# Split k weight copies, three more filler matmuls, a new load order and new issue lists in a fused attention and gMLP block

## Chip, core and metric

One NeuronCore of a Trainium2 chip runs the whole program. The metric is the device time of one execution in microseconds, here the median of several executions. The profile is of one more execution, read as time from the first to the last instruction of the program (the span).

## What is computed

The input x is 2048 tokens by 448 features in bf16. A pre-norm attention block is followed by a pre-norm gMLP block, each with a residual sum:

```python
qkv = layernorm(x) @ wqkv                 # 16 heads of 28
idx = pos[:, None] - 2 * arange(8)        # each token sees 8 tokens, 2 apart
o   = softmax(q . k[idx] * 28**-0.5, masked where idx < 0) . v[idx]
h   = x + o @ wo
z   = gelu(layernorm(h) @ w_in)           # 1792 wide: z1 and z2, 896 each
g   = w_sp @ layernorm(z2) + b_sp         # w_sp mixes the 2048 tokens
out = h + (z1 * g) @ w_out
```

## The kernel before, in words

Tokens lie in 16 blocks of 128. Blocks u and u+8 form unit u, so there are eight units, worked from 7 down to 0. One half of the partitions of `xh` holds the features of the low tokens and the other half those of the high ones, so most matmuls run as pairs on 64 rows each.

The stages, with the lines of the profile:

- **First layernorm** (`ln_unit`, L647 to L710): `bn_stats` and `bn_aggr` per block on DVE (L656, L657), the root `rs1_u` on POOL (L646, L647) or ACT (L668, L669), the normalised blocks `nrm1_b` into `tring` on DVE (L676). Units 7, 6 and 5 are transposed by PE (`tT1_u`, L692, seven matmuls) and copied to `xh` (`ev1_u`, L641 or L643). Units 4 to 0 are transposed by DMA (`tD1_u`, L683).
- **Weights of q and k**: loaded into a staging area in `z2p` and copied into `wpd` with 32 columns a head (`cpq`, `cpk`, L641 on ACT, L643 on DVE). v needs only the copies `cpv` between partition halves.
- **Projections and attention**: `mmq`, `mmk` (L783, chunks 3, 2, 1, 0 of 128, 128, 256 and 512 tokens), `mmv` (L823), logits `mml` (L858), row sums `mmr` (L886), values `mmo` (L911), output projection `mmy` (L964).
- **gMLP**: `mmz2` (L984), `mmz1` (L1028), the mixing over tokens `g` (L1064, nearly half of PE's time), the output `wo` (L1093).

The order of work is not that of the source. The functions add about 680 tasks, and a table of numbers, `SEQ`, gives for each engine (SP, POOL, DVE, ACT, PE) the list of its tasks. `Planner.replay` walks the five lists, hands out PSUM banks and buffers and emits the instructions. Semaphore waits follow from what each task reads and writes, so a change of a list changes what stands behind what on an engine, and which PSUM banks a task gets. DMAs are issued from SP's list and, at the start, from ACT's.

Two things ahead of the projections matter below. `c_warm` (L614) fills the operand of the filler matmuls `f0` (L635), which keep PE busy until the first transposes; `c_wo0` (L627) clears the area of the output weights. Both run on DVE.

The planner keeps a count of PE instructions, two for each matmul (a weight load and the matmul), since PE's instructions arrive in blocks. The count at which a block is asked for and the one at which it must be there are written so:

```python
CHUNK, ASK, NEED = 256, 118, 434
...
a, b = self.CHUNK * len(self.asks) + self.ASK, self.CHUNK * self.k_need + self.NEED
```

Block boundary k therefore stands at PE instruction 434 + 256 k, which is matmul 217 + 128 k, and its block is asked for 158 matmuls earlier.

Of the kernel before, what the change touches and what calls it, by code (L numbers as in the profile page):

```python
# [32 lines left out]

SCALE = DH ** (-0.5)
SEQ = (
# [30 lines left out]
)  # L66
NBANKS = 8
NE = 2
# [310 lines left out]
def bass_sequential_preLN__sliding_local_dilated__mixer_gmlp__prompt_kernel(  # L379
# [18 lines left out]
    with contextlib.ExitStack() as top:  # L398
# [71 lines left out]
        r_st = {p: [Res("st%s%d" % (p, n)) for n in range(2)] for p in "kqv"}  # L470
# [159 lines left out]
        def fill(name, n, deps=()):  # L630
            fb = []

            def em():
                for _ in range(n):
                    iss("pe", lambda e: e.matmul(psum[:, fb[0] * 512:fb[0] * 512 + 512], warm[:, 0:128], warm[:, :]),  # L635
                        reads=[r_warm], writes=[r_bank[fb[0]]])
            return add(name, "pe", 0.216 * n, em, deps=[c_warm] + list(deps), acq=[("ps", 1, fb)], rel=[("ps", fb)], mode="F", nmm=n)
# [12 lines left out]
        def ln_unit(u, which, src_deps, ev_deps):  # L650
# [11 lines left out]
            def em_r():  # L662
# [4 lines left out]
                else:  # L667
                    iss("act", lambda e: e.activation(dst, var, AF.Ln, bias=epst[:, 0:1]), reads=rr + [r_eps], writes=rr)  # L668
                    iss("act", lambda e: e.activation(dst, dst, AF.Exp, scale=-0.5), reads=rr, writes=rr)  # L669
            tr = add("rs%d_%d" % (which, u), "pool", 1.1, em_r, deps=tb + [c_nhalf, c_eps],  # L670
                     epoch=0 if which == 1 else None, alts={"pool": 1.1, "act": 0.36} if which == 1 else None)
            tk.append(tr)
            tn, h = [], []
            for n, b in enumerate(bl):
# [32 lines left out]
        for u in range(NU - 1, -1, -1):  # L707
# [3 lines left out]
                               [r_xh[NU - 1]], [r_xpad[1]])], 0.2, eng="dve", deps=[t_xh[NU - 1]])  # L711

        fill("f0", 15)
        c_kpad = cst("c_kpad", [(lambda e: e.memset(kT[:, :, :, HALO + ST:XW], 0.0), [], [r_kend]),
                                (lambda e: e.memset(kT[:, 0, :, 0:HALO], 0.0), [], [r_kh]),
                                (lambda e: e.memset(qT[:, :, :, 0:2], 0.0), [], [r_qend]),
# [22 lines left out]

        t_cp = {}  # L740
        for p in "kq":
            for j in range(2 if p == "q" else 1):
                nh = 8 if p == "q" else 16
                for n, (h, q) in enumerate(((0, 0), (0, 1), (1, 0), (1, 1))):
                    tk = []
                    nb = 4 - q
                    ne = nb * nh * DH

                    def em(p=p, h=h, q=q, j=j, n=n, nb=nb, nh=nh, tk=tk):
                        copy(tk[0].eng, wpd[p][64 * h:64 * h + 64, q:NC7:2, 256 * j:256 * j + 32 * nh].rearrange("p c (h d) -> p c h d", d=32)[:, :, :, 0:DH],  # L750
                             w_st[p][64 * q:64 * q + 64, 0:nb, 224 * j:224 * j + nh * DH].rearrange("p c (h d) -> p c h d", d=DH),
                             r_st[p], [r_w[p][j][n]] if p == "q" else [r_w[p][0][n], r_w[p][1][n]])
                    t = add("cp%s%d%d%d" % (p, j, h, q), "dve", dve4x(ne), em, deps=t_w[p] + [c_wp[p]], alts={"dve": dve4x(ne), "act": act_c(ne)})
                    tk.append(t)
                    for jj in ((j,) if p == "q" else (0, 1)):
                        t_cp.setdefault((p, jj), []).append(t)
        t_cp["v", 0] = cross("cpv", wv, r_w["v"], t_w["v"], D)

# [405 lines left out]
```

## Time and profile before

| | us |
|---|---|
| median of 3 executions | 242.88 |
| lowest and highest | 242.75, 243.28 |
| the profiled execution, its own time | 242.73 |
| its span | 240.9 |
| PE busy, of the span | 233.1 (97%) |
| DVE busy | 140.3 (58%) |
| ACT busy | 96.1 (40%) |
| POOL busy | 26.9 (11%) |

The profiled execution is 0.15 us under the median. Its own time stands 1.8 us over its span. To read it: the time is the time at which PE starts real work, plus PE's stream, plus PE's gaps, plus the last addition and store. A gap of PE is put down in the profile to the engine that ended it, or to "issue" when it waited for nothing that the profile shows.

### The profile page before, as it was taken

The page shows a single profiled execution, that of the slowest core. Times are in us where ns is not written, and L with a number is a line of the kernel's source. Part 1 is how long each engine was busy: PE and PEld are TensorE (multiplying, and loading weights), DVE is VectorE, ACT ScalarE, POOL GpSimd, SP SyncE. Part 2 cuts the span into 40 slices and gives each one's busy share as a digit, 9 for nine tenths or more (in the row PEclk, how much of TensorE's full clock was granted, in tenths as well). Part 3 has the DMA queues.
Part 4 walks back from the last instruction along what each step waited for, and adds up shares of the span by engine and source line. Part 5 has one row for each costly group of instructions (what it writes and reads, how often), then busy time and mean ns, then how long its engine had stood idle before and what let it go on. Part 6 is the DMA issues. An engine that isn't in the chain of part 4 may idle for free.

```text
span 240.9 us, 6695 instructions
## 1 busy us (share of the span) xinstructions
PE 233.1 (97%) x3009; PEld 119.9 (50%) x3019; DVE 140.3 (58%) x280; ACT 96.1 (40%) x113; POOL 26.9 (11%) x66
## 2 busy tenths in 40 slices
PE   7898999999999999999999999999999999999995
PEld 2486865456554544554444444444444444444453
DVE  5999959378999899788810050253101436554443
ACT  2996988889899947764730000000000000000000
POOL 4062000002014321304600000000000000000000
PEclk9999999999999999999999999999999999999999
DMA  7949575574213557987632733350000000010122
GB/s 213 337 106 103 112 125 95 97 127 53 44 22 77 109 85 174 169 133 117 141 76 58 174 68 65 85 46 0 0 0 3 0 0 19 20 60 0 38 93 78
DMA packets 54628, 20.01 MB, mean 83 GB/s; under 512 B 46792, under 2 KB 54472, under 8 KB 54600
## 3 DMA queue, kind: packets, MB, share of 16 engines
q1 hardware_dynamic: 53496, 18.67, 39.6%
q10 hardware_dynamic: 1104, 0.92, 1.3%
q8 instruction: 23, 0.38, 0.7%
q14 instruction: 5, 0.04, 0.1%
HBM read 6.37 MB, written 1.84 MB: 34 GB/s over the span
## 4 chain that ended last, share of the span: by engine, by line
PE 88%; DVE 5%; DMA 2%; issue 1%; POOL 1%; ACT 1%; SPq 0%
PE psum L1064 40%; PE psum L783 11%; PE psum L1093 9%; PE psum L984 8%; PE psum L964 5%; PE psum L823 5%; PE psum L1028 4%; PE psum L858 2%; PE psum L911 2%; DMA x_tm<-in_A_x_dram 2%; DVE z2p L1014 2%; PE psum L886 1%; DVE st L1000 1%; DVE tring L676 1%; POOL rs L647 1%
## 5 line engine op out<-in xcount | busy, mean ns | idle before, releaser
L1073 DVE TENSOR_TENSOR ub<-psum,reg 128x512 bf16<-128x512 f32 x28 | 18.9, 687 | 68.7 <-PE psum L1064 66.4
L1064 PE MATMUL psum<-reg,z2p 128*128 128x512 bf16 x220 | 49.4, 379 | 0.2
L1064 PE MATMUL psum<-wspT_lo,z2p 128*128 128x512 bf16 x218 | 48.5, 379 | 0.4 <-DVE z2p L1014 0.2
L1064 PEld LDWEIGHTS psum<-wspT_lo,z2p 128*128 128x128 bf16 x224 | 21.8, 98 | 26.6 <-issue 0.4
L1064 PEld LDWEIGHTS psum<-reg,z2p 128*128 128x128 bf16 x224 | 21.9, 98 | 26.2
L783 PE MATMUL psum<-xh,reg 64*128 64x128 bf16 (+2 forms) x448 | 26.0, 270 | 0.2
L1093 PE MATMUL psum<-reg 128*128 128x448 bf16 (+2 forms) x119 | 22.2, 341 | 0.1
L984 PE MATMUL psum<-w_in,xh 64*128 64x448 bf16 x224 | 22.2, 349 | 0.0
L1028 PE MATMUL psum<-xh,w_in 64*128 64x512 bf16 x196 | 21.8, 376 | 0.0
L641 ACT ACTIVATE reg<-psum 128x896 bf16<-128x896 f32 (+2 forms) x25 | 20.0, 844 | 1.9 <-PE psum L783 1.0
L783 PEld LDWEIGHTS psum<-xh,reg 64*128 64x128 bf16 x448 | 16.8, 94 | 7.8 <-issue 0.8
L656 DVE BATCH_NORM_STATS2 st<-x_tm 128x6 f32<-128x448 bf16 x32 | 19.6, 612 | 1.4 <-DMA x_tm<-in_A_x_dram 1.2
L1000 DVE BATCH_NORM_STATS2 st<-z2p 128x6 f32<-128x448 bf16 x32 | 17.5, 611 | 3.1 <-ACT z2p L994 3.1
L870 ACT ACTIVATE reg<-psum 128x928 bf16<-128x928 f32 x18 | 16.2, 939 | 4.1 <-PE psum L858 4.1
L646 POOL TENSOR_SCALAR rs<-mv 128x2 f32<-128x2 f32 x19 | 7.5, 393 | 88.4 <-DVE mv L657 70.2
L1038 ACT ACTIVATE reg<-psum 128x1024 bf16<-128x1024 f32 x14 | 13.6, 1029 | 8.0 <-PE psum L1028 8.0
L1093 PEld LDWEIGHTS psum<-reg 128*128 128x128 bf16 x119 | 11.4, 98 | 10.4
L994 ACT ACTIVATE z2p<-psum 128x896 bf16<-128x896 f32 x16 | 14.2, 916 | 5.6 <-PE psum L984 5.6
L1103 DVE TENSOR_TENSOR tring<-psum,x_tm 128x448 bf16<-128x448 f32 (+2 forms) x17 | 10.1, 596 | 10.2 <-PE psum L1093 10.1
L984 PEld LDWEIGHTS psum<-w_in,xh 64*128 64x128 bf16 x224 | 10.6, 94 | 10.4 <-issue 0.4
L929 DVE TENSOR_TENSOR reg<-psum,reg 128x912 bf16<-128x912 f32 x9 | 11.1, 1235 | 7.2 <-ACT reg L921 6.6
L1028 PEld LDWEIGHTS psum<-xh,w_in 64*128 64x128 bf16 x196 | 9.5, 94 | 11.5
(63 smaller groups left out, 205.9 us busy)
## 6 DMA issues: line engine op xcount, KB each, us to landing
x_tm<-in_A_x_dram SPq DMA_DIRECT2D x15, 112.0 KB, 4.2
out_dram<-tring SPq DMA_DIRECT2D x15, 112.0 KB, 1.7
w_in<-in_B_w_in_dram SPq DMA_DIRECT2D x2, 448.0 KB, 4.5
reg<-in_B_w_out_dram SPq DMA_DIRECT2D x1, 784.0 KB, 6.0
z2p<-in_A_wqkv_dram ACTq DMA_DIRECT2D x2, 336.0 KB, 4.5
reg<-in_B_b_sp_dram SPq DMA_DIRECT2D x1, 512.0 KB, 4.6
w_in<-in_B_w_in_dram SPq DMA_DIRECT2D x2, 224.0 KB, 4.3
reg<-in_A_wo_dram SPq DMA_DIRECT2D x4, 98.0 KB
```

The lines of the kernel that those rows point to most:

```text
L641: iss("act", lambda e: e.activation(dst, src, AF.Copy), reads=rd, writes=wr)
L656: iss("dve", lambda e: e.bn_stats(st[:, b, :], x_tm[:, b, :]), reads=[r_x[b]], writes=[rl[b]])
L783: iss("pe", lambda e, c=c, s=s, gi=gi, lhs=lhs: e.matmul(psum[:, bk[s] * 512 + cw * gi:bk[s] * 512 + cw * gi + cw], lhs, xh[64 * s:64 * s ...
L870: iss("act", lambda e: e.activation(E[:, es[0], 2 * n:2 * n + 2, :], pair_view(lb, 0, 8 * JW), AF.Exp, scale=SCALE), reads=[r_bank[lb[0]], ...
L984: iss("pe", lambda e, k2=k2, c=BLK[s][k2], s=s: e.matmul(psum[:, zb[s] * 512:zb[s] * 512 + D], xh[64 * s:64 * s + 64, c, HX + 128 * u:HX + ...
L994: iss("act", lambda e: e.activation(z2p[:, u:u + 9:8, D * k:D * k + D], pair_view(zb, 0, D), AF.Gelu_apprx_tanh), reads=[r_bank[zb[0]], r_ ...
L1000: iss("dve", lambda e, b=b: e.bn_stats(st3[:, b, k, :], z2p[:, b, D * k:D * k + D]), reads=[r_z2[b][k]], writes=[r_st3[b][k]])
L1028: iss("pe", lambda e, k=k, c=BLK[s][k], s=s: e.matmul(psum[:, bk[s] * 512:bk[s] * 512 + 512], w_in[64 * s:64 * s + 64, k, 128 * f:128 * f ...
L1038: iss("act", lambda e: e.activation(z1p[f].rearrange("p (s t) -> p s t", s=2)[:, :, 512 * ch:512 * ch + 512], pair_view(bk, 0, 512), AF.Ge ...
L1064: iss("pe", lambda e, b=b: e.matmul(psum[:, gb[0] * 512:gb[0] * 512 + 512], z2p[:, b, 128 * f:128 * f + 128], src[:, b, 512 * (tc % 2):512 ...
L1073: iss("dve", lambda e: e.tensor_tensor(ub[:, us_[0], :], psum[:, gb[0] * 512:gb[0] * 512 + 512], bb[:, 512 * tc:512 * tc + 512], ALU.add), ...
L1093: iss("pe", lambda e, f=f: e.matmul(psum[:, wb[0] * 512 + d0:wb[0] * 512 + d1], z1p[f][:, 128 * m:128 * m + 128], w_out[:, f, d0:d1], star ...
```

## The change

Four edits in the source, and new lists.

1. The copies of k's weights. Before, all four copies (two halves h, two staging halves q) took 16 heads at once. Now the two with q = 0, which cover all four column blocks, still do; the two with q = 1 are split into eight heads each. So k has six copies instead of four, and a projection of groups 2 and 3 no longer waits for the other half's copy.
2. A task `f1` of three filler matmuls behind the transposes of unit 7.
3. The planner's cost of a root on ACT, 0.36 to 0.54, which only the planner sees.
4. `SEQ` is replaced as a whole (the task numbers shift by one to three).

```diff
-    (28, 31, 26, 24, 29, 27, 25, 55, 87, 48, 85, 73, 86, 330, 384, 366, 348, 402, 420, 438, 341, 456, 395, 359, 413, 467,
...
+    (24, 29, 26, 31, 27, 28, 25, 41, 88, 48, 87, 55, 67, 86, 79, 73, 351, 333, 387, 369, 405, 423, 441, 459, 344, 398, 434,
...
-                     epoch=0 if which == 1 else None, alts={"pool": 1.1, "act": 0.36} if which == 1 else None)
+                     epoch=0 if which == 1 else None, alts={"pool": 1.1, "act": 0.54} if which == 1 else None)
...
         fill("f0", 15)
+        fill("f1", 3, [pl.named["tT1_7"]])
...
         for p in "kq":
-            for j in range(2 if p == "q" else 1):
-                nh = 8 if p == "q" else 16
-                for n, (h, q) in enumerate(((0, 0), (0, 1), (1, 0), (1, 1))):
+            for n, (h, q) in enumerate(((0, 0), (0, 1), (1, 0), (1, 1))):
+                whole = p == "k" and q == 0
+                for j in range(1 if whole else 2):
+                    nh = 16 if whole else 8
...
-                             r_st[p], [r_w[p][j][n]] if p == "q" else [r_w[p][0][n], r_w[p][1][n]])
+                             r_st[p], [r_w[p][0][n], r_w[p][1][n]][j:j + nh // 8])
...
-                    for jj in ((j,) if p == "q" else (0, 1)):
+                    for jj in range(j, j + nh // 8):
                         t_cp.setdefault((p, jj), []).append(t)
```

What the lists move, on PE at three places. The rows are groups of equal instructions in the order in which PE has them; the last number of a row is the count of matmuls. Lines behind L692 are up to three higher in the changed kernel, so L823 is L826 and so on.

PE from its first instruction, before:

```order
L635 MATMUL psum<-warm 128x512 x15
L692 MATMUL psum<-ident,tring 128x128 x14
L783 MATMUL psum<-xh,reg 128x128 x28
L823 MATMUL psum<-reg,xh 64x448 x56
L783 MATMUL psum<-xh,reg 128x128 x196
L692 MATMUL psum<-ident,tring 128x128 x7
L858 MATMUL psum<-reg 64x58 x96
L823 MATMUL psum<-reg,xh 64x448 x28
```

The same place in the changed kernel:

```order
L636 MATMUL psum<-warm 128x512 x15
L693 MATMUL psum<-ident,tring 128x128 x7
L636 MATMUL psum<-warm 128x512 x3
L693 MATMUL psum<-ident,tring 128x128 x7
L786 MATMUL psum<-xh,reg 128x128 x28
L826 MATMUL psum<-reg,xh 64x448 x56
L786 MATMUL psum<-xh,reg 128x128 x112
L693 MATMUL psum<-ident,tring 128x128 x7
L786 MATMUL psum<-xh,reg 128x128 x84
L826 MATMUL psum<-reg,xh 64x448 x28
L861 MATMUL psum<-reg 64x58 x64
```

The three fillers stand between the transposes of units 7 and 6. Unit 5's transposes moved ahead of the last 84 projection matmuls, and the v projection of unit 6's tile (x28) now stands ahead of the first logits instead of behind 96 of them. Boundary 1, matmul 345, lies in the logits before and in that v projection now.

PE where the queries of the 512-token chunk and the values of tiles 6 and 5 meet, before:

```order
L783 MATMUL psum<-xh,reg 128x512 x42
L886 MATMUL psum<-reg,ones 32x464 x8
L911 MATMUL psum<-reg 32x58 x32
L886 MATMUL psum<-reg,ones 32x464 x8
L911 MATMUL psum<-reg 32x58 x32
L783 MATMUL psum<-xh,reg 128x512 x28
L964 MATMUL psum<-reg 128x448 x8
L911 MATMUL psum<-reg 32x58 x64
```

and in the changed kernel:

```order
L786 MATMUL psum<-xh,reg 128x512 x28
L889 MATMUL psum<-reg,ones 32x464 x16
L786 MATMUL psum<-xh,reg 128x512 x14
L914 MATMUL psum<-reg 32x58 x128
L786 MATMUL psum<-xh,reg 128x512 x14
L826 MATMUL psum<-reg,xh 64x448 x28
L861 MATMUL psum<-reg 64x58 x64
L967 MATMUL psum<-reg 128x448 x8
```

The values of the two tiles (L914) now run as one group of 128, with one 512-token group on each side. Boundary 7, matmul 1113, falls behind 112 of these 128.

PE around the output projections of units 4 to 2, before:

```order
L823 MATMUL psum<-reg,xh 64x448 x28
L964 MATMUL psum<-reg 128x448 x8
L886 MATMUL psum<-reg,ones 32x464 x8
L911 MATMUL psum<-reg 32x58 x64
L858 MATMUL psum<-reg 64x58 x64
L984 MATMUL psum<-w_in,xh 128x448 x14
L964 MATMUL psum<-reg 128x448 x8
```

and in the changed kernel:

```order
L967 MATMUL psum<-reg 128x448 x8
L889 MATMUL psum<-reg,ones 32x464 x8
L914 MATMUL psum<-reg 32x58 x16
L826 MATMUL psum<-reg,xh 64x448 x28
L914 MATMUL psum<-reg 32x58 x64
L861 MATMUL psum<-reg 64x58 x64
L967 MATMUL psum<-reg 128x448 x8
L861 MATMUL psum<-reg 64x58 x64
L967 MATMUL psum<-reg 128x448 x8
L889 MATMUL psum<-reg,ones 32x464 x8
L987 MATMUL psum<-w_in,xh 128x448 x14
```

The output projections (L967) stand between the logits groups instead of behind them. Boundary 12, matmul 1753, falls behind 30 of the first 64 logits shown here, and boundary 13, matmul 1881, behind 6 of the 14 matmuls of L987; before, boundary 13 fell into the last L964 row.

On the other engines, in words. DVE runs `c_wo0` ahead of `c_warm` now, and the last `nrm1` of the first layernorm come ahead of the masks and of the copies of k and q out of PSUM. The root of unit 6 moved from ACT to POOL. ACT's first three copies of q are `cpq000`, `cpq100`, `cpq011`, and `cpv` changed places (`cpv0` to ACT, `cpv1` to DVE). The first five loads of SP and the five of ACT are the ones of before; all others on SP are in a new order, and the two large pieces of `w_in` now stand behind most of x instead of among it. On ACT, the first gelu no longer stands between the last exponentials, so two table loads are gone. In the last half of the program (L1064 on) only the first dozen groups differ in order.

59 rows, old and new, of the table SEQ are left out of this document.

## The prediction, as put on record

> **What bounds the kernel now.** I read the page's busy shares first, then PE's waits, then the chain that ended last, then PE's timeline around each gap.
>
> ```profile
> PE 233.1 (97%) x3009; PEld 119.9 (50%) x3019; DVE 140.3 (58%) x280; ACT 96.1 (40%) x113; POOL 26.9 (11%) x66
> ...
> q8 instruction: 23, 0.38, 0.7%
> ```
>
> PE is busy in 97% of the span, so only three things can move the time: when PE's stream starts, what is in it, and its gaps. The second row is a DMA queue that carries instructions: 23 packets, 0.38 MB. PE's records, 3009 matmuls and 3019 weight loads, make 6028 instructions, or 262 to a packet.
>
> The next rows are PE's waits (engine and line, what ended the wait, us, times, longest), then the chain in order of time (start, length, what).
>
> ```profile
> PE psum L858 <- issue: 0.9, 1, 0.9
> PE psum L964 <- DVE mv L657: 0.8, 1, 0.8
> ```
>
> ```profile
> 16.52 0.15 issue
> 16.66 2.63 PE psum L783 x88
> 19.30 0.50 PE psum L692 x7
> 19.79 0.37 PE psum L858 x32
> 20.16 0.87 issue
> ...
> 46.29 3.19 PE psum L783 x28
> 49.48 1.62 PE psum L964 x8
> 51.10 0.61 PE psum L911 x64
> 51.71 0.64 PE psum L858 x61
> 52.35 0.26 issue
> ```
>
> ```profile
> 67.36 1.69 PE L964 MATMUL psum<-reg 128*128 128x448 bf16 x8
> 68.98 0.39 PE L886 MATMUL psum<-reg,ones 64*32 64x464 bf16 x8
> 69.18 0.73 PE L911 MATMUL psum<-reg 64*32 64x58 bf16 x64
> 69.85 0.83 PE L858 MATMUL psum<-reg 32*64 32x58 bf16 x64
> 70.61 1.50 PE L984 MATMUL psum<-w_in,xh 64*128 64x448 bf16 x14
> 72.86 1.69 PE L964 MATMUL psum<-reg 128*128 128x448 bf16 x8 [0.75 <-DVE mv L657]
> ```
>
> Four gaps in mid-stream: 0.15 at 16.5, 0.87 at 20.2, 0.26 at 52.4 and 0.75 at 72.1, together 2.03 us. Summing the order's counts, they stand at matmul 221, 348, 1240 and 1878. The kernel's own count puts block boundaries at matmul 217 + 128 k: 217, 345, 1241 and 1881 for k = 0, 1, 8 and 13. All four fit within four matmuls, so I read all of them as **PE waiting for its next block of instructions**. The fourth is put down to DVE `mv`, the statistics of block 13, which L964 of unit 2 doesn't read.
>
> How long must PE work between asking (158 matmuls ahead) and the boundary so as not to wait? The work plus the gap tells. k = 1: 119 matmuls of L783 (2.63/88 each, 3.56), 0.50, 0.37 and 0.15 of the first gap make 4.58; with 0.87, **5.45 needed**. k = 13: 67.36 to 72.11 is 4.75; with 0.75, 5.50. k = 8: 22 of 28 (2.51) + 1.62 + 0.61 + 0.64 = 5.38; with 0.26, 5.64. Less sufficed at k = 4, in this piece of the chain:
>
> ```profile
> 26.75 3.21 PE psum L783 x56
> 29.96 0.32 PE psum L886 x8
> 30.28 0.55 PE psum L911 x64
> 30.83 2.77 PE psum L823 x56
> ...
> 131.28 10.74 PE psum L1064 x49
> ```
>
> 13 of 56 (0.75), 0.32, 0.55, 2.77, another row of 8 (0.32) and 9 of 64 (0.08) make 4.79, and no gap. (The last row, 0.22 for a matmul of 512 columns, is for the fillers below.) So the need lies between under 4.79 and 5.64.
>
> On the rule: the Trainium skill, Runtime: NRT & Kernel Launch, Instruction fetch mechanics, says that instructions come in 16 KiB blocks of 256, and that crossing a block boundary is "mostly hidden". The trace agrees on the size (262 by the records) and not on the hiding, 0.87 at one of them. By that rule the gaps would have another cause and stay; that time is rival 1's.
>
> **The change part by part.**
>
> *Boundaries.* The windows of 158 matmuls in the new order, by the rows above: k = 0: 101 of L783 at 0.030 (3.0) and 56 of L823 (2.77), 5.8. k = 1: 41 + 84 of L783 (3.7), 0.50, 26 of 28 of L823 (1.3), **5.5 where it was 4.6**. k = 13: twice 64 of L858 (1.28), 16 of L964 (3.24), 8 of L886 (0.3), 6 of L984 (0.6), 5.4 where it was 4.75. k = 8: 46 of L911 (0.4), 14 of L783 (1.6), 28 of L823 (1.4), 64 of L858 (0.64), 6 of L964 (1.2), 5.2. Two grow shorter: k = 7 (16 + 14 of L783, 3.4, 16 of L886, 0.4, 112 of L911, 1.0) 4.8, and k = 12 (8 + 4 of L911 and L964, 1.7, L886 0.3, 28 of L823 1.4, 80 of L911 0.75, 30 of L858 0.3) 4.5. So the 2.03 us go, and come back in part: k = 7 between 0 (need under 4.79) and 0.85 (need 5.64), k = 12 between 0 and 1.1, k = 8 between 0 and 0.4. For k = 12 I take 0.2: like k = 4 it lies where few transfers run. For k = 7 0.2 and for k = 8 0.1, near the row without a gap. **Minus 2.03, plus 0.5**, with 0 and 2.35 as ends.
>
> *Changes of form.* By the planner's mode of each task the array's form changes 48 times before and 54 times after. A group of 32 of L858 takes 0.37 and one of 64 takes 0.64, so 0.10 is the entry. Six more: **plus 0.6**, with ends 0 (work behind hides it) and 0.9 (0.15 each, the shortest gap above, should an entry cost that).
>
> *Start.* PE's timeline (brackets hold the idle time ahead and what ended it; the second row is the last four fillers alone), then DVE's:
>
> ```profile
> 1.51 5.95 PE L635 MATMUL psum<-warm 128*128 128x512 bf16 x15 [1.51 <-DVE warm L614]
> 6.17 1.28 PE L635 MATMUL psum<-warm 128*128 128x512 bf16 x4
> 7.92 0.56 PE L692 MATMUL psum<-ident,tring 128*128 128x128 bf16 x7 [0.47 <-DVE tring L676]
> 9.04 0.56 PE L692 MATMUL psum<-ident,tring 128*128 128x128 bf16 x7 [0.56 <-DVE tring L676]
> ```
>
> ```profile
> 0.96 0.48 DVE L614 MEMSET warm<- 128x512 bf16 x1 [0.96 <-PEq L1149]
> 1.58 0.81 DVE L627 MEMSET reg<- 128x896 f32 x1
> ```
>
> The two memsets change places, so the fillers start 0.9 later, at 2.4. Eleven took 6.17 - 1.51, 0.42 each, and the rest runs towards the 0.22 of L1064: the clock steps up late in them. They end at 7.46, 0.46 ahead of the transposes. If the step comes at the same moment, two slow fillers fewer fit ahead of it and run at 0.22 behind it, and they end at about 7.9: nothing lost. If it comes 0.9 later too, they end at 8.4. Three more fillers of 0.22, 0.66, lie in a gap of 0.56. **Plus 0.1**, ends 0 and 0.55.
>
> The root of unit 6 goes to POOL:
>
> ```profile
> 114.55 0.38 POOL rs L646
> 114.93 0.07 issue
> 115.00 0.88 POOL rs L647
> ```
>
> The pair takes 1.33. Between the statistics and `nrm1_6` DVE has four instructions of the size of `nrm1` (1.13 for three, in a row below), 1.5 us. They hide it; nothing, and up to 0.4 if POOL is slowed.
>
> *Copies of k, copies of q and v.* Two more instructions, on ACT. DVE's pairs are the cover:
>
> ```profile
> 10.94 1.48 DVE L643 COPY reg<-z2p 64x1792 bf16<-64x1792 bf16 x2
> ```
>
> A joint copy is 0.74. Splitting two of them and handing three of the four halves to ACT frees about 0.4 on DVE and loads ACT with about 1 us, ahead of L783 of groups 2 and 3 of k, which PE reaches at about 16, a little later than before. So nothing; 0.3 if ACT is late.
>
> *Loads.* The first five of SP stay, so the first statistics get their data as before; 0. The later blocks of x come earlier, which DVE doesn't wait for; that also leaves less in the DMA engines when blocks 0 and 1 are fetched.
>
> *Transposes by DMA.* The queries of the 512-token chunk need units 0 to 3. Their PE place moves ahead by 28 matmuls of L823 (1.4) and 64 of L911 (0.55), and the first two gaps are gone (1.0): from 34.5 to about 31.5.
>
> ```profile
> 24.62 1.13 DVE L676 TENSOR_SCALAR tring<-x_tm,mv,rs 128x448 bf16<-128x448 bf16 x3 [0.62 <-ACT rs L669]
> ...
> 26.70 1.22 DVE L643 CAST reg<-psum 128x1024 bf16<-128x1024 f32 x1
> ...
> 28.13 1.12 DVE L877 TENSOR_TENSOR reg<-reg,mband 128x1856 bf16<-128x1856 bf16 x1
> 29.17 0.39 DVE L676 TENSOR_SCALAR tring<-x_tm,mv,rs 128x448 bf16<-128x448 bf16 x1
> ```
>
> ```profile
> 29.59 1.22 SPq L683 DMA_TRANSPOSE xh<-tring  x1
> ```
>
> ```profile
> DMA to landing us min/median/max: 2.9/3.0/6.2
> ```
>
> The last `nrm1` moves ahead of the cast and the mask (2.3) and loses the 0.62, but gains one copy of w_in and a pad (about 1.2): 29.6 less 1.7 is 27.9 for its end. With 3.0 to landing, 30.9, 0.6 ahead of PE. Nothing, up to 1.0 if one lands late (4.5).
>
> *The rest.* Two fewer table loads on ACT, and new order among the gelus and nrm3: PE's chain there shows no wait for either but 0.2 at the first L1064, which I keep.
>
> **The sum.** -2.03 + 0.5 + 0.6 + 0.1 = **-0.8** on the profiled execution's 242.73 (its span 240.9 and 1.8 around it), 241.9. The median lies 0.15 higher: 242.1. Forecast's own range 241.4 to 242.4.
>
> **Rivals.**
>
> 1. *The block waits come back.* Blocks 7, 8 and 12 are asked for while transposes of w_sp or of xh hold the DMA engines, as at k = 8 before, and cost 0.85 + 0.4 + 1.1 = 2.35: -2.03 + 2.35 + 0.7 = +1.0, **243.9**. From 1.85 us of returned gaps on the kernel is slower by 0.5. For it: these windows are shorter than 5.64. Against: k = 4 got by with 4.79.
> 2. *The fillers stay slow.* If the clock's step follows the fillers by the same time instead, they end at 8.4 and everything moves by 0.45, and the three fillers and a transpose run at half speed for part: +0.45 to +1.2, **242.6 to 243.3**, about 242.8. For it: 0.42 for the first eleven against 0.22 later. The Trainium skill, TensorE: Matmul & The Clock Gate, Part 1, has the gate watch a free-running window of 3.4 us, so the step would vary from run to run; no row here can show that.
> 3. *The transposes for the query chunk land late*: +0.6, **242.7**. For it: the issue rows are 2 us apart and a landing took up to 6.2. Against: 0.6 of slack.
>
> **How the numbers follow.** Forecast 0.54, rival 1 0.18, rival 2 0.15, rival 3 0.13. Range 241.3 to 243.4: the forecast's low end with all gaps gone, up to rival 2's high end; most of rival 1 is what it leaves out. A difference of 0.2% is 0.5 us, about what a measurement tells from none, so faster is below 242.4: 0.52 (nearly all of the forecast); slower is above 243.4: 0.18 (rival 1 with what lies above 2's end); the same is 0.30.
>
> **What would show it.** Right: no "issue" idle near 16.5, 20 and at the boundary behind L987; PE's busy time up by about 1.2. Wrong: "issue" or unexplained idle at matmul 1113, 1241 or 1753; L692 starting after 8.2; L786 of 512 columns waiting for DMA at about 31.5.

## The result, and the profile after

The kernel became slower, not faster: median **244.9 us** (242.9 to 246.6, 13 executions) against 242.63 for the kernel before (13 executions beside it). The ratio is 1.0071, 95% interval 1.0046 to 1.0095. A second set of executions of the changed kernel gave 1.0094 (1.0059 to 1.0129); together about 1.008, or 2.0 us. Predicted were 242.1, in a range of 241.3 to 243.4. Of the 21 executions of both sets 7 show a mean granted clock of 0.992 or 0.993 and have a median of 245.9, the 14 at full clock one of 244.3; of 114 of the kernel before 2 show it.

The profiled execution took 244.31 us, its span is 242.6 (before: 242.73 and 240.9). Busy time and the instruction queue, as before:

```profile
PE 233.9 (96%) x3012; PEld 122.9 (51%) x3022; DVE 142.7 (59%) x282; ACT 92.0 (38%) x105; POOL 28.0 (12%) x72
...
q8 instruction: 23, 0.38, 0.7%
```

PE is busy for 0.8 us more and the span is 1.7 longer, so some 0.9 is new idle time. (Matmul lines are three higher than before.) PE's waits, then the rows of the chain at the waits:

```profile
PE psum L636 <- DVE warm L615: 2.4, 1, 2.4
PE psum L914 <- issue: 1.5, 2, 1.1
PE psum L861 <- issue: 1.2, 2, 1.1
PE psum L693 <- DVE tring L677: 0.2, 1, 0.2
```

```profile
31.60 4.71 PE psum L786 x42
36.31 0.61 PE psum L914 x64
36.92 0.59 PE psum L861 x51
37.51 1.07 issue
...
46.37 1.01 PE psum L914 x112
47.37 1.11 issue
...
69.19 0.17 issue
...
77.96 0.40 issue
```

None of the four gaps of before is there: no wait at k = 0, 1, 8 or 13. But four others are: 1.07 at matmul 857 (k = 5), 1.11 at 1113 (k = 7), 0.17 at 1751 (k = 12), 0.40 at 2006 (k = 14), together 2.75 us where before had 2.03.

The start is earlier, not later:

```profile
2.45 5.26 PE L636 MATMUL psum<-warm 128*128 128x512 bf16 x15 [2.45 <-DVE warm L615]
7.66 0.56 PE L693 MATMUL psum<-ident,tring 128*128 128x128 bf16 x7
8.06 0.81 PE L636 MATMUL psum<-warm 128*128 128x512 bf16 x3
8.79 0.56 PE L693 MATMUL psum<-ident,tring 128*128 128x128 bf16 x7
```

The second transposes begin at 8.79 (before 9.04): in this trace the blocks of x came earlier, and the three fillers fit in the gap.

What does a block wait for? The trace's record of queue q8 gives the start of each packet; the time of asking is PE's at the planner's count, and no trace records it. Block 5 is asked for at 32.0 (matmul 699) and its packet starts at 36.24, 4.2 later; block 7 is asked for at 42.3 and starts at 45.46, 3.1 later. With nothing in the DMA engines it can be 1.1 (k = 11: asked for at 60.3, start at 61.41), but also 2.2 (k = 12: 64.5 and 66.71, DMA share 0.00 in between). From the packet's start to the first matmul of its block it took 2.3 to 3.3 us wherever PE waited. SP's queue at that time:

```profile
32.73 1.17 SPq L949 DMA_TRANSPOSE wspT_lo<-in_B_w_sp_dram  x1
33.95 0.59 SPq L589 DMA_DIRECT2D w_in<-in_B_w_in_dram  x1
35.79 1.85 SPq L949 DMA_TRANSPOSE wspT_lo<-in_B_w_sp_dram  x1
37.69 0.59 SPq L589 DMA_DIRECT2D w_in<-in_B_w_in_dram  x1
39.20 1.17 SPq L949 DMA_TRANSPOSE wspT_lo<-in_B_w_sp_dram  x1
40.41 1.04 SPq L589 DMA_DIRECT2D w_in<-in_B_w_in_dram  x1
42.87 1.16 SPq L949 DMA_TRANSPOSE wspT_lo<-in_B_w_sp_dram  x1
```

Each w_sp load lands just ahead of the next (35.78, 39.18, 42.85, 48.34), and the large piece of w_in at 45.06. Packet 5 starts 0.5 after the landing at 35.78, packet 7 0.4 after that at 45.06. That made the first theory: **a block waits behind loads in the DMA engines**. Two things speak against it as it stands: from 33.4 to 34.2 the DMA share is 0.11 and packet 5 does not start, and packet 7 starts while the engines are full (1.03 from 45.0 to 45.4). Rivals: a block needs a fixed stretch of work, or the new order is slower by itself (forms).

### The profile page after: what moved, and what is told of

Read it like the earlier page. It is cut to its first block, busy times and chain, and to the rows that moved or that the text cites. A ratio compares the mean times of both kernels' runs of the same rounds, so it can differ in the third digit from the quotient of the medians.

```text
span 242.6 us, 6705 instructions
## 1 busy us (share of the span) xinstructions
PE 233.9 (96%) x3012; PEld 122.9 (51%) x3022; DVE 142.7 (59%) x282; ACT 92.0 (38%) x105; POOL 28.0 (12%) x72
## 3 DMA queue, kind: packets, MB, share of 16 engines
HBM read 6.37 MB, written 1.84 MB: 34 GB/s over the span
## 4 chain that ended last, share of the span: by engine, by line
PE 91%; DVE 3%; issue 2%; DMA 2%; POOL 1%; SPq 0%; POOLq 0%
PE psum L1067 40%; PE psum L987 9%; PE psum L786 9%; PE psum L1096 9%; PE psum L1031 9%; PE psum L967 5%; PE psum L826 4%; PE psum L861 3%; PE psum L914 2%; DMA x_tm<-in_A_x_dram 2%; PE psum L889 1%; DVE tring L677 1%; DVE st L657 1%; DVE reg L644 1%; POOL rs L648 1%
## 5 line engine op out<-in xcount | busy, mean ns | idle before, releaser
L987 PE MATMUL psum<-w_in,xh 64*128 64x448 bf16 x224 | 22.8, 349 | 0.0
L642 ACT ACTIVATE reg<-psum 128x512 bf16<-128x512 f32 (+2 forms) x22 | 17.7, 831 | 5.9 <-PE psum L786 3.8
L1003 DVE BATCH_NORM_STATS2 st<-z2p 128x6 f32<-128x448 bf16 x32 | 18.0, 607 | 2.9 <-ACT z2p L997 2.8
L987 PEld LDWEIGHTS psum<-w_in,xh 64*128 64x128 bf16 x224 | 12.1, 94 | 9.4 <-issue 1.0
L647 POOL TENSOR_SCALAR rs<-mv 128x2 f32<-128x2 f32 x22 | 6.7, 302 | 87.0 <-DVE mv L658 70.8
L648 POOL TENSOR_TENSOR rs<-rs,nhalf 128x2 f32<-128x2 f32 x22 | 16.3, 740 | 1.8
L1031 PEld LDWEIGHTS psum<-xh,w_in 64*128 64x128 bf16 x196 | 11.1, 94 | 9.8 <-ACT reg L1041 0.2
```

Of the source, the lines that this page charges most:

```text
L642: iss("act", lambda e: e.activation(dst, src, AF.Copy), reads=rd, writes=wr)
L648: iss("pool", lambda e: e.tensor_tensor(dst, dst, nh, ALU.pow), reads=rr + [r_nhalf], writes=rr)
L987: iss("pe", lambda e, k2=k2, c=BLK[s][k2], s=s: e.matmul(psum[:, zb[s] * 512:zb[s] * 512 + D], xh[64 * s:64 * s + 64, c, HX + 128 * u:HX + ...
L1003: iss("dve", lambda e, b=b: e.bn_stats(st3[:, b, k, :], z2p[:, b, D * k:D * k + D]), reads=[r_z2[b][k]], writes=[r_st3[b][k]])
L1031: iss("pe", lambda e, k=k, c=BLK[s][k], s=s: e.matmul(psum[:, bk[s] * 512:bk[s] * 512 + 512], w_in[64 * s:64 * s + 64, k, 128 * f:128 * f ...
```

## The experiments

All ratios are to the kernel before, run beside them on the same chip; 0.001 is 0.24 us.

**1. Loads held back.** Two loads wait for PE, and those behind them in SP's list with them (the three pieces of w_in now stand ahead of the w_sp loads).

```diff
+        for load, work in (("win0_2", "mml6_01"), ("wsp0_15", "mmo5_3")):
+            w = pl.named[work]
+            w.mark = []
+            pl.named[load].deps.append(w)
+            pl.named[load].waits.append(w)
         chain([t_wsp[b][0] for b in S_ORDER], t_xh[0])
```

> The changed kernel with seven loads of the middle stretch held back, nothing else: the three loads of the first half of w_in wait for PE's matmul 865 (just behind boundary 5), four transposed loads of w_sp wait for matmul 1129 (behind boundary 7), so that no transposed load runs between about 33 and 48 us. Theory (a block of instructions comes late because it waits behind loads in the DMA engines): blocks 5 and 7 start soon after they are asked for (1.1 to 2 us instead of 3.1 to 4.2), the issue waits of 1.07 at matmul 857 and 1.11 at 1113 go, and the time falls by 1.5 to 2.2 us, to 242 to 243. Rival 1 (a block needs some 5.5 us of work ahead whatever the DMA engines do): both waits stay within 0.3 us, no change. Rival 2 (the loss is the new order itself, its form changes and small idle times): the waits may go, but the time stays within 0.3 us.

1.0037 (1.0014 to 1.0060), median 243.57: about 1 us won back, less than expected. Blocks 5, 6 and 8 start 1.4, 1.1 and 1.1 after they are asked for, block 7 2.0, and neither wait is left. But the profiled execution, with 245.57 the slowest of the 12, shows one that was not there:

```profile
PE psum L786 <- issue: 1.8, 1, 1.8
PE psum L861 <- issue: 0.5, 1, 0.5
PE psum L914 <- issue: 0.4, 1, 0.4
```

The 1.8 stands at 31.5, ahead of the first queries of the 512-token chunk, where no block boundary is: the last `xh` transpose landed at 33.17, and PE went on at 33.37.

**2. Boundaries moved by 36 matmuls.**

```diff
-                for _ in range(n):
-                    iss("pe", lambda e: e.matmul(psum[:, fb[0] * 512:fb[0] * 512 + 512], warm[:, 0:128], warm[:, :]),
+                for i in range(n):
+                    w = 128 if name == "f0" and i < 12 else 512
+                    for c in range(0, 512, w):
```

> The changed kernel with twelve of the fifteen first fillers split into four matmuls of 128 columns each: the same columns, 36 more matmuls ahead of all work, so every block boundary falls 36 matmuls earlier in the work. Theory (PE waits at the boundaries, and the lists are laid around their places): by the trace of the changed kernel the windows of work for a need of 5.5 us then fall short by 9.8 us in all instead of 1.3, or by 7.5 if the need is 4.1 where no load runs; the time rises by 5 to 8.5 us, to 249 to 253, with issue waits at matmuls 217 + 128 k counted with the fillers. Rival (the boundaries cost little, the time follows from the order and the forms): within 0.3 us of the changed kernel.

1.0126 (1.0098 to 1.0154), 245.32: by the ratios some 1 us above the changed kernel, by the medians (244.9 and 245.23) hardly, where 5 to 8.5 were expected. The rule of a fixed need fell here: in its trace block 6 is asked for 3.85 us before it is used and PE does not wait (its packet starts 1.12 after the ask); blocks 8, 9, 11 and 12 get by with 4.4 to 4.7 and at most 0.2 of wait. So the 5.45 to 5.64 of the prediction are no fixed need. They are not simply what blocks needed that met loads, either: at k = 13 of before the DMA engines were empty (share 0.00 from 67.4 to 70.0) while the block was waited for.

**3. Without f1**, `fill("f1", 0, ...)`.

> The changed kernel without the three fillers f1 between the first transposes. Theory of the boundaries: each falls three matmuls later in the work, and by the trace's windows the shortfall goes from 1.3 to 1.8 us: 0.2 to 0.7 us slower than the changed kernel. Rival (the fillers themselves cost time at the start): 0.2 to 0.6 us faster. Rival (fillers keep the clock up): the stretch behind them at half clock, 1 to 2 us slower, shown by matmuls of the k projections at twice their 0.030 us.

1.0139 (1.0101 to 1.0178), 246.16, more than expected, so the fillers are not the loss. Its trace has 1.7 at block 7 and 1.3 for `xh`; why it is over 1 us slower than the changed kernel stays open.

**4. Before, boundaries moved by nine** (the edit of 2, with `i < 3`).

> The kernel before with three of its fifteen fillers split into four of 128 columns: the same columns, nine more matmuls ahead, boundaries nine matmuls earlier in the work. Theory: by the trace of before the windows then fall short of 5.5 us by 4.4 us in all instead of 5.9 (3.4 instead of 4.2 where 4.1 is enough without loads), so 0.7 to 1.4 us faster than before, 241.2 to 241.9. Rival (boundaries cost little): within 0.2 us of before.

Wrong: 1.0041 (1.0017 to 1.0065), 243.75. The profiled execution shows one block wait, 1.1 at k = 13, where before has four of 2.03, and was with 242.17 the fastest of 12. One trace shows one draw.

**5. The changed kernel again.**

> The changed kernel itself, for a second trace and more times. Theory: 244 to 245 us; in the trace either the 512-token queries at matmul 695 start at 31.6 and PE waits about 1 us for block 5 at matmul 857, as in the first trace, or they wait 1 to 2 us for the last xh transpose and then the wait at 857 is gone, because block 5 arrives meanwhile. Rival (the two waits are independent): both together, or neither, with the same time.

1.0094, as above, median 245.23. The second trace, of the slowest of these executions (246.59), is the other case that was expected. PE's timeline, and a window of 4 us (PE's, PEld's, DVE's, ACT's and POOL's busy time and counts, the granted clock, the DMA share, GB/s):

```profile
30.82 0.70 PE L914 MATMUL psum<-reg 64*32 64x58 bf16 x64
33.65 6.40 PE L786 MATMUL psum<-xh,reg 64*128 64x512 bf16 x42 [2.13 <-issue]
39.97 0.68 PE L914 MATMUL psum<-reg 64*32 64x58 bf16 x64
```

```profile
34.00:38.00 4.00, 4.00 (x26) 1.77 (x22) 1.51 (x2) 0.00 (x0) 0.00 (x0) 0.57 0.83 87
```

PE waits 2.13 for the last `xh` transpose, and then the clock is granted at half for some 3.4 us: the 42 matmuls take 6.40 instead of the 4.71 of the first trace. Behind that no wait at 857, since block 5 came meanwhile; 1.0 at k = 7 and 0.5 at k = 14 stay. By the terms: -2.03 + 2.13 + 1.69 + 1.5 + 0.8 (forms) - 0.2 (start) is +3.9; the span, 244.9, is 4.0 longer than before's. A loss of 1.7 us is 0.007 of the span, which fits the executions with a clock of 0.993; that all of them lose it here is not shown. The five first `xh` transposes, this execution then the first:

```profile
DMA to landing us min/median/max: 3.0/4.4/6.0
```

```profile
DMA to landing us min/median/max: 3.1/4.0/4.6
```

Of eight traces that have these queries in this place, five show a wait of 1.2 to 2.1 there, of six with the list of before none. In those five the last transpose is issued at 28.3 to 28.7 (27.5 in the first trace) and lands 4.5 to 5.1 later, and PE goes on 0.2 behind the landing.

**6. Blocks 12 and 14 freed as well**: `("wsp0_5", "mml1_01")` as a third pair in 1, and SP's list so (the w_sp loads of the second half also go behind those of the first):

```diff
-    tD2_7 wsp0_13 tD2_6 wsp0_4 tD2_4 wsp0_12 tD2_5 wsp0_3 w_out tD2_3 wsp0_11
+    tD2_7 wsp0_5 tD2_6 tD2_4 wsp0_13 tD2_5 wsp0_4 w_out tD2_3 wsp0_12 wsp0_3
```

> The changed kernel with the loads held as in the run with the middle stretch held back, and the transposed loads of w_sp also taken out of the way of boundaries 12 and 14: one of the four goes out only behind matmul 1755, the two after it behind the transposes of xh that boundary 14 waits beside; the w_sp loads of the second half go behind those of the first. Theory (a block waits behind transposed loads in the DMA engines): on top of what the first hold gave, the issue waits of 0.3 to 0.5 at matmuls 1753 and 2006 go as well: 242.2 to 242.9 us, so 1.5 to 2.2 below the changed kernel; no issue wait of over 0.2 between matmul 857 and 2009. Rival (form changes and small idle times of the new order carry the loss): within 0.3 us of the first hold, 243.0 to 243.8. Rival (the w_sp loads become late themselves): a wait of L1067 for a load at about 120 us, 244 or more.

Not one block wait is left, and the time is that of the changed kernel: 1.0093 (1.0065 to 1.0121), 245.31.

```profile
PE psum L786 <- ACT reg L902: 1.2, 1, 1.2
PE psum L693 <- DVE tring L677: 1.0, 2, 0.7
PE psum L987 <- DMA xh<-tring: 0.9, 1, 0.9
PE psum L1067 <- DVE ub L1076: 0.8, 1, 0.8
```

The loads that went out of the way met the second set of `xh` transposes (0.9 at 96 us). Only the third rival came near, at another place than it named.

**7. Before, with three early loads later** in SP's list:

```diff
-    x1 wo1 win1_2 x3 x8 wo0 tD1_4 x0 wo3
+    x1 x3 x8 tD1_4 x0 win1_2 wo3
...
-    wsp0_7 win1_1
+    wsp0_7 wo1 wo0 win1_1
```

> The kernel before with three early loads put later: two pieces of w_o behind the first load of w_sp (30 us) and a piece of w_in behind the last x block (18.5 us), so that they are not in the DMA engines when blocks 0 and 1 are fetched. Theory: block 1 starts at most 2 us after it is asked for instead of 2.9, the waits of 0.87 at matmul 348 and 0.15 at 221 go: 0.5 to 1.0 us faster than before, 241.7 to 242.2. Rival (a block's delay has nothing to do with the loads): within 0.2 us of before, the 0.87 stays.

Packet 1 starts 1.2 after the ask (2.9 before), and the waits at 221 and 348 are gone, as expected. But the edit cannot have the credit: in the traces of 10 and 13, where these loads stand as before, packet 1 starts 1.3 and 1.6 after the ask, and both waits are missing too. Nor were loads in the way in the trace of before, where packet 1 is asked for at 15.4 and starts at 18.31 (a window's columns are those of 5, the DMA share last but one):

```profile
15.00:16.00 1.00, 1.00 (x44) 1.00 (x38) 0.96 (x4) 0.98 (x3) 0.80 (x4) 1.00 0.05 7
16.00:17.00 1.00, 0.85 (x33) 0.73 (x29) 0.97 (x4) 0.99 (x2) 0.76 (x3) 1.00 0.04 14
17.00:18.00 1.00, 1.00 (x43) 1.00 (x38) 0.92 (x4) 0.91 (x3) 0.85 (x3) 1.00 0.00 0
```

The time is 1.0008 (0.9985 to 1.0032):

```profile
PE psum L692 <- DVE tring L676: 1.4, 2, 0.8
PE psum L964 <- DVE mv L657: 0.7, 1, 0.7
PE psum L858 <- DVE reg L643: 0.6, 1, 0.6
PE psum L823 <- issue: 0.4, 1, 0.4
```

PE is 1.2 us earlier at 22 us and gives it back: 0.8 at 39 us behind an eviction on DVE (the 0.6), the rest in small waits, 0.3 of it at blocks 8 and 10.

**8. All parts but the lists**: the changed program with the `SEQ` of before and the new tasks put in.

```diff
-    tT1_7 ... cpk001 ... cpk011
+    tT1_7 f1 ... cpk001 cpk101 ... cpk011 cpk111
```

> All parts of the change but the lists: the program of the changed kernel with the lists of before, the two new k copies placed right behind the ones they were split from, f1 behind its transpose. Theory (the loss comes from the order in the lists, through block waits and form changes): within 0.4 us of before, 242.4 to 243.1; boundaries fall three matmuls earlier in the work, which moves the waits of before little. Rival (fillers or split copies cost): 1 us or more slower than before, with PE waiting in the first 20 us.

1.0026 (1.0001 to 1.0051), 243.31, just above what was expected. So about two thirds of the loss is the lists', with an interval of 0 to 1.2 us for the rest. Its trace does not show that rest in PE: the last matmul ends at 238.49 (238.33 before), and the span's other 0.95 stand behind it, where the last store lands 2.54 after its issue (1.59 before).

**9. and 10. Plain loads of w_sp**, in the changed kernel and in that of before.

```diff
-                dst[:, b, :], B_w_sp[1024 * half:1024 * half + 1024, 128 * b:128 * b + 128], transpose=True),
+                dst[:, b, :], B_w_sp[128 * b:128 * b + 128, 1024 * half:1024 * half + 1024]),
```

> The changed kernel with the 32 loads of w_sp as plain loads instead of transposed ones: the same bytes into the same places at the same points of SP's list, but not transposed, so the spatial product is of another matrix; nothing else. Theory (blocks of instructions and the xh transposes wait behind the transposed w_sp loads): blocks 5, 6, 7, 12 and 14 start 1 to 2 us after they are asked for, no wait of 1 us at matmuls 857 and 1113: 1.5 to 2.5 us faster than the changed kernel, 242.4 to 243.4. What is left against before is then form changes (0.8) and the wait for xh at matmul 695. Rival (any load of these bytes delays blocks as much): the issue waits stay, time within 0.5 of the changed kernel.

> The kernel before with the same edit: plain loads of w_sp. Theory: its waits at k = 0 and 1 are before the first w_sp load and stay (1.0), the one at k = 8 goes (0.2), the one at k = 13 has no w_sp load beside it and stays (0.9): 0 to 0.5 us faster than before, 242.1 to 242.6, so the distance of the two kernels shrinks from about 2 us to about 0.8. Rival (the new order is slower by itself): the distance stays at about 2.

1.0028 (1.0004 to 1.0052) and 0.9986 (0.9971 to 1.0001): the distance shrinks from 2.0 to 1.0 us. But plain loads delay blocks too: packet 7 still starts 4.0 after the ask, beside the piece of w_in, and costs the 1.4 of this row; packet 8 of before starts 3.3 after.

```profile
PE psum L914 <- issue: 1.4, 1, 1.4
```

So plain loads delay a block as well, not the transposing alone. In the kernel of before the waits at k = 0 and 1, which were to stay, are missing, and the one at k = 8, which was to go, is there beside that at k = 13:

```profile
PE psum L964 <- DVE mv L657: 0.6, 1, 0.6
PE psum L823 <- issue: 0.3, 1, 0.3
```

All 17 traces together (the first 16 blocks of each) give a weaker form of the theory. Where the DMA engines were busy under 3% from the ask to the packet's start (72 blocks), the start came after 1.0 to 3.2 us, 1.8 in the mean; where they were busy over 50% (145 blocks), after 1.05 to 4.2, 2.5 in the mean. Loads lengthen the delay, and it was over 3.2 only beside them. What sets it when the engines are empty stays open.

**11. The 512-token queries later**, in PE's list and in ACT's:

```diff
-    mmo8_3 mmq0_0 mmk0_2 mmk0_1 mmo7_0 mmo7_1 mmo7_2 mmo7_3 mml5_00 mml6_00 mml5_01
+    mmo8_3 mmo7_0 mmo7_1 mmo7_2 mmo7_3 mml5_00 mml5_01 mmq0_0 mmk0_2 mmk0_1 mml6_00
...
-    rex8 evk0_2 evk0_1 exp5_0
+    rex8 exp5_0 evk0_2 evk0_1
```

> The changed kernel with 96 matmuls moved ahead of the first group of queries of the 512-token chunk (L914 of block 7 and half of L861 of block 5, with one exponential moved on ACT), so that the group comes 1.2 us later, at about 32.8. Theory (PE waits there for the last xh transpose in most executions, and a wait of about 2 us there halves the clock for 3.5 us): the wait for xh shrinks to under 0.5, no execution has a granted clock of 0.993, a wait of 0.3 to 1.5 for block 4 stands at matmul 729 in its place, the one at 857 goes: 0.5 to 1.2 us faster than the changed kernel, 243.5 to 244.2. Rival (the wait for xh was chance and is not part of the loss): as the changed kernel or slower by the wait for block 4.

1.0070 (1.0037 to 1.0103), 244.21: as the first set of the changed kernel. No wait for `xh`; block 4 waits instead, as expected, but the sum of the waits is the same:

```profile
32.94 0.30 PE L914 MATMUL psum<-reg 64*32 64x58 bf16 x29 [1.11 <-issue]
```

And 3 of 10 executions have a clock of 0.993, so that expectation failed; where they lose it no trace shows.

**12. 1 and 11 together.**

> The run before this one, with the loads of the middle stretch held back as in the first experiment. Theory (waits for xh and waits for blocks are both fed by the same DMA engines, and together they are the loss beyond the form changes): both wait for xh and the waits at 857 and 1113 are gone: 242.4 to 243.3, within 0.7 us of before. Rival (one wait only takes the place of another): 243.5 to 244.5, no better than either edit alone.

1.0055 (1.0027 to 1.0082), 243.62: no better than the hold alone, as the rival has it. The waits at 857 and 1113 are gone; 0.8 at block 4, 0.4 for `xh` and 0.6 at block 14 are left, and 3 of 12 executions have a clock of 0.986 to 0.993.

**13. Ten more changes of form in the kernel before**, by six exchanges like these in PE's list:

```diff
-    mmo7_3 mmv5 ... mmv2 mmr8 ... mmo8_3 mmk0_0
+    mmv5 mmo7_3 ... mmr8 mmv2 ... mmk0_0 mmo8_3
```

> The kernel before with six neighbours exchanged in PE's list (the last part of L911 of block 7 with L823 of block 5, L823 of block 2 with L886 of block 8, the last L911 of block 8 with the first L783 behind it, the last L858 of blocks 5 and 6 with the L783 behind it, the last L911 of block 6 with the first L858 of block 4, the last L911 of block 1 with L984 behind it): the same work, ten more changes of the array's form (58 instead of 48), boundaries at nearly the same work. Theory (a change of form costs about 0.14 us, by the sums over all changes in the traces of before and of the changed kernel, 7.8 us for 46 and 8.6 for 52): 0.8 to 1.8 us slower than before, 243.4 to 244.4; the six more of the change then account for 0.5 to 1.0 of its loss. Rival (work behind hides an entry): within 0.3 us of before, and the order's remaining loss has another cause.

1.0015 (1.0000 to 1.0030): +0.36 us, near the rival. Summing over all changes of form in the trace (from the last matmul of one form to the first of the next, less the usual distance, waits left out) gives 9.4 us where before has 7.8, 0.16 an entry; another choice of the usual distance (the median distance in the group that follows) gives 10.0 and 8.0. A second way needs no such choice: PE's time from the first projection to the last matmul, less its waits over 0.1. It is 227.5 here, 226.7 in the mean of the five other traces with the list of before (226.5 to 227.0), and 227.3 in the mean of the nine full-clock traces with the list of the changed kernel (227.0 to 227.9). So ten entries cost some 0.8, and the new order 0.6. But in this trace, of the fastest execution (242.00), the block waits are smaller:

```profile
PE psum L911 <- issue: 0.2, 1, 0.2
PE psum L964 <- ACT reg L870: 0.2, 1, 0.2
```

Most of that is not the edit's doing: packets 0 and 1 started 2.6 and 1.6 after the ask instead of 3.4 and 2.9, with nothing edited ahead of them. That the time which PE spends on entries is taken off the wait for a late block is not shown.

**14. 1 with two changes of form fewer**, in PE's list:

```diff
-    mmy6 mml3_00 mml3_01 mml3_10 mml3_11 ... mmy5 mml2_11
+    mml3_00 mml3_01 mml3_10 mml3_11 mmy6 ... mml2_11 mmy5
```

> The changed kernel with the loads of the middle stretch held back as in the first experiment, and two neighbours of PE's list exchanged so that two changes of form fall away (52 instead of 54: L967 of unit 6 behind the last L861 of block 3, L967 of unit 5 behind the last L861 of block 2). Theory: 0.2 to 0.4 us below the first hold, so 242.7 to 243.5; still above before, since the waits at boundaries 12 and 14 and the wait for xh stay. Rival: no different from the first hold.

1.0076 (1.0046 to 1.0106), 243.84, no gain; its trace again has 1.4 for `xh`. With 1 and 12 it puts the worth of the hold at 0 to 1 us, no closer.

**15. 1, 9 and 11 together.**

> The changed kernel with all three edits that thinned out its waits: plain loads of w_sp (the same bytes, not transposed, so the spatial product is of another matrix), the loads of the middle stretch held back, and 96 matmuls ahead of the first group of 512-token queries. Theory (the loss is waits for blocks and for xh, fed by the DMA engines, and a rest of 0.4 to 0.8 from six more changes of form): no wait of over 0.9 in the trace, 242.3 to 243.2. Rival (a loss that these edits don't touch): 243.4 or more, no better than plain loads alone.

**1.0018 (1.0000 to 1.0037)**, 242.64, and all 12 executions at full clock. Two waits over 0.2 are left behind the fillers:

```profile
PE psum L914 <- issue: 0.8, 1, 0.8
PE psum L786 <- DVE reg L644: 0.3, 1, 0.3
```

The 0.8 stands at matmul 685, where no boundary is. So about 1.5 of the 2.0 us go when the loads are thinned out and PE doesn't run into them: waits for blocks and for `xh`, and the clock lost after the long ones. 0.45 is left. Plain loads take 0.3 off the kernel before as well (10); measured against that, 1.2 go and 0.8 is left. No version that transposes w_sp beats the kernel before.

## Why the prediction was wrong

- **The step that failed: "-2.03 plus 0.5", above all the 0.5.** k = 7 was taken at 0.2 and measured 1.11, k = 12 at 0.2 and 0.17, k = 8 at 0.1 and 0; k = 5 and k = 14 were not in the sum and cost 1.07 and 0.40. Returned were 2.75, above the upper end of 2.35 and past the 1.85 from which rival 1 was to make the kernel slower. The ground: I took the need, 4.79 to 5.64 us, for a property of the work between ask and boundary. It is the time until the packet starts (1.0 to 4.2 us) and some 2.6 behind it. So block 14 had 6.1 us of work and waited all the same, and block 6 in 2 had 3.85 and did not wait. The first part is longer beside loads, and the changed kernel has some beside the asks of blocks 5 and 7: with them held back (1) these blocks start 1.4 and 2.0 after the ask instead of 4.2 and 3.1, and PE waits for neither. I costed the new load order at 0 and laid it only against the statistics that read the loads, not against the times at which blocks are asked for. What else sets the first part I can't say.
- **"Like k = 4 it lies where few transfers run"**, the reason for the 0.2 at k = 12, was a misreading: in the trace of before the DMA share is 0.88 from 29.0 to 33.8, between ask and use of block 4.
- **The -2.03** held in the first trace, where all four gaps are gone. But half of it, the 1.02 at k = 0 and 1, is missing as well in the two traces whose early program is that of before (10 and 13). It was one draw and was priced as certain.
- **Rival 1** was right in kind and near in the waits (2.35 for 2.75), with two of its three places wrong; its time, +1.0 to 243.9, was half of the loss. Chance given: 0.18.
- **"Nothing" for the `xh` transposes** failed as well, in most traces. The slack of 0.6 was right for a landing of 3.0 (30.9 forecast, 30.63 in the first trace); later issues and landings of 4.5 to 5.1 made it a wait of 1.2 to 2.1. Rival 3 priced it at 0.6 and left out the clock: after 1.84 and 2.13 of idling PE ran at half clock, another 1.7; after 1.1 to 1.69 (3, block 7) it did not. The Trainium skill, TensorE: Matmul & The Clock Gate, Part 1, has the gate close after an idle window of about 3.4 us; here 1.84 was enough, and the measurement decides.
- **Forms, 0.6**: the six changes cost 0.8 by the same sum (7.8 for 46 changes, 8.6 for 52; 1.4 by the other choice in 13) and 0.6 by PE's time without its waits, so about as forecast.
- **Start, 0.1**: -0.25 in the first trace, which is a draw too: the first projection begins at 9.36 to 10.16 in the eleven traces with the new list and at 9.39 to 9.69 in the six with that of before. Rival 2 did not happen.
- **POOL and the k copies, 0**: no wait for the k copies. The 0.2 at 16.7 ends a chain through a root that POOL finished at 15.93, within the 0.4 allowed.
- By the rows the first trace is -2.03 + 2.75 + 0.8 - 0.25 + 0.2 (the transposes at 16.7) = +1.5 against 1.6 measured; the executions that lose clock lift the median above it. What the 0.45 to 0.8 left in 15 is was not separated, though the 0.6 of the new order would cover most of it; nor why 8 lost its 0.6.

## What to carry to other kernels

Where an engine's instructions stream in, a load can hold up the next block: lay the issue and landing of the loads against the times at which blocks are asked for, not only against their readers, and leave room, since a block's delay varied by 2 us even with empty DMA engines. A wait that is removed often stood in for the next one, so price it by the sum of the waits that are left in the stretch. And where waits hang on the landing of DMAs, one trace is one draw: look at two or three before a term is taken at zero, or a wait in the kernel before is taken as sure to be won.

## What the hardware showed that was not expected

- The same block of the same kernel started 4.0 and 1.8 us after it was asked for (k = 4, the two traces of the changed kernel); from the packet's start to use it was always 2.1 us or more.
- With the DMA engines empty (share 0.00) blocks started 1.1 us after the ask (k = 11 of the changed kernel) and 2.2 us after it (k = 12), in one trace.
- The Trainium skill, Runtime: NRT & Kernel Launch, Instruction fetch mechanics, calls the crossing of a block boundary "mostly hidden". In these traces it is so only with 4 to 6.8 us of work ahead of it; waits were up to 1.7.
- Idle times of 1.84 and 2.13 us on PE were each followed, 0.6 and 0.4 us after PE had started again, by half clock over 3.41 us; one of 1.69 us was not.
